# A recurrence with an FFN behind it on one core: v's first product on 128 rows, late transposes by DMA, and a new order of work

## The chip, the core and the metric

The kernel runs on one core of a Trainium2 chip. The core has TensorE (PE in the profile; its weight loads are PEld), VectorE (DVE), ScalarE (ACT), GpSimd (POOL) and SyncE (SP), and 16 DMA engines. The metric is the device time of one execution in microseconds; the median of several runs is compared.

## The reference

Inputs r, k, v, w, a, b are [4 batches, 8 heads, 768 steps, 40], float32. For each of the 32 heads a 40 x 40 state runs through the steps, and its readings go through a feed-forward network (FFN) with 320 inputs, 2048 hidden units and a squared relu:

```python
for t in range(S):
    y[:, :, t] = np.einsum('bhd,bhde->bhe', rt, state)
    Sa = np.einsum('bhde,bhe->bhd', state, at)
    state_decay = state * wt[:, :, None, :] - np.einsum('bhd,bhe->bhde', Sa, bt)
    state = state_decay + np.einsum('bhd,bhe->bhde', vt, kt)
...
h = x @ w_in            # x: y of all heads side by side, [3072, 320]
r = np.maximum(h, 0.0)
return (r * r) @ w_out
```

## The kernel before

The 768 steps are cut into 12 chunks of 64 (`L`, `NCH`). Inside a chunk the recurrence is written as products of 64 x 64 triangles, so that only one small state passes from chunk to chunk. Steps or features of two heads, or of two halves of the heads (g = 0 and 1), share the 128 partitions. For each chunk c the functions run in this order:

- `load(c)` brings w, k, b, a, v and r from HBM on SP's queue (`ldw`, `ldk`, `ldb`, `lda`, `ldv`, `ldr`), in pieces of 160 KB. Chunk 0 also loads the FFN's weights in pieces (`lwi`, `lwl`, `lwo`), which `cwi`, `cwl`, `cwo` cast.
- `prep(c)` takes the logarithm of w (`ln`), splits it (`hi`, `lo`), sums it over the steps on TensorE (`ci`, `cf`) and takes exponentials (`ei`, `ex`, `ef`). `mulKB` scales k and b into the tile KB. `castV` puts v into one half of the rows of VU; u comes into the other half later. `TK` turns KB on TensorE into PSUM and `tK` evicts it into KBT; `TA` and `TR` do so for a and r (tile AR). The triangle `EN` is a product of KBT and AR, and `mEN` masks it into the tile EN (line 689).
- `rec(c)` is the chain from chunk to chunk: `AS` (a times the state) and `EV` (EN times v) add up in one PSUM bank, `u0` evicts it to NZ, `NU` multiplies EN by NZ, `u1` evicts u into VU, `S` and `SC` make the new state and `s` scales it into STb (line 781). `TS` turns the state and `tS` evicts it into Sb, which only the reading of the next chunk needs. EV reads 64 rows of EN and of VU at a time, those that hold v.
- `read(c)` turns VU (`TV`, evicted by `tV` into VUT), makes the triangle `CX` and its masked form `mCX`, adds `RS` (r times Sb) and `Y`, scales the result (`y`, `yd`) and turns it (`XT`, `xt`).
- `ffn(c)` makes h in four parts u (`F` and `FL`), evicts with relu (`f`, lines 928 and 930), squares (`q`) and multiplies by WOUT (`O`), evicts (`o`) and stores (`st`) on SP's queue.

A transpose is a TensorE product with an identity, by `tp` (line 394) or, for the chunks in `WHOLE`, by `tpw` (line 397) on 128 x 128 blocks; all other products are recorded at line 390. Evictions go through `copy_alts` (lines 371 to 380).

The order of the work is not found at run time. `plan.add` collects the operations with what they read and write, and `plan.issue(ORDER)` emits them one by one as the text `ORDER` says, each with its engine (`ACT f 0 u1`) and, on TensorE, the PSUM slot (`PE2 EV 0`, one of four). Every engine runs its own instructions in that order, and waits for the data or for the buffer of an instruction that is not done. A DMA is issued by the engine on whose queue it stands: SP for nearly all, ScalarE for half of the first load and two of the last stores.

Of the kernel before, what the change touches and what calls it, by code (L numbers as in the profile page):

```python
# [8 lines left out]
BF16 = mybir.dt.bfloat16  # L9
# [77 lines left out]
ORDER = """SP ldw 0; SP ldk 0; SP ldb 0; SP ldw 1; ACT ln 0; DVE hi 0; DVE lo 0; SP lda 0; PE0 cf 0; POOL  # L87
castB 0; SP ldk 1; POOL castK 0; ACT eg 0; PE1 TK 0; SP ldb 1; ACT ln 1; PE2 ci 0; DVE tK 0 g0;
ACT ef 0; SP ldv 0; DVE tK 0 g1; POOL hi 1; ACT exw 0; ACT castA 0; SP lda 1; DVE lo 1; PE1 TA 0;
ACT castB 1; PE2 ci 1; SP ldw 2; DVE tA 0 g1; DVE tA 0 g0; PE0 EN 0 g1; ACT exw 1; PE1 cf 1; POOL  # L90
castV 0 g1; DVE mEN 0 g1; ACT castK 1; SP ldr 0; POOL castV 0 g0; PE2 EN 0 g0; ACT ef 1; PE3 BK 0;
DVE mEN 0 g0; SP ldb 2; ACT castA 1; SP lda 2; PE2 EV 0; DVE bK 0; PE0 TA 1; ACT u0 0; SP ldv 1;
DVE tA 1 g1; ACT eg 1; PE NU 0; PE3 TK 1; POOL castR 0; ACT u1 0 g0; DVE tK 1 g0; ACT ln 2; PE1 TR
0; ACT u1 0 g1; POOL hi 2; DVE tA 1 g0; SP lwi 0 k1 x2; ACT tRw 0; POOL lo 2; DVE tK 1 g1; SP ldk
2; PE2 EN 1 g0; PE0 TV 0; ACT castB 2; DVE mEN 1 g0; POOL castA 2; SP ldw 3; PE3 S 0 g0; ACT tV 0;
PE S 0 g1; PE1 EN 1 g1; POOL castV 1 g1; DVE s 0 q0; PE2 BK 1; DVE s 0 q1; ACT castV 1 g0; PE0 ci
2; SP lwi 0 k0 x2; DVE mEN 1 g1; PE3 CX 0 g1; SP lwi 0 k1 x1; ACT exw 2; SP ldr 1; ACT castK 2;
DVE mCX 0 g1; PE0 cf 2; PE1 TK 2; ACT eg 2; SP lwi 0 k0 x3; PE3 AS 1; ACT ef 2; PE EV 1; SP lwi 0
k1 x0; DVE tK 2 g1; SP lwi 0 k0 x0; ACT bK 1; PE0 TS 0; DVE u0 1; SP lwi 0 k1 x3; SP lwi 0 k0 x1;
DVE tK 2 g0; ACT ln 3; PE NU 1; SP ldv 2; ACT tS 0; PE2 CX 0 g0; POOL hi 3; DVE mCX 0 g0; PE1 TA  # L100
2; POOL lo 3; SP lwl 0; ACT u1 1 g0; PE0 SC 1; DVE tA 2 g1; ACT u1 1 g1; PE S 1 g0; PE2 Y 0; DVE
tA 2 g0; POOL castR 1; SP ldk 3; PE S 1 g1; DVE y 0; PE3 TR 1; PE1 EN 2 g1; DVE yd 0; ACT tRw 1;
DVE s 1 q0; POOL cwi 0 k1h0; PE2 EN 2 g0; DVE mEN 2 g1; PE3 TV 1; POOL cwi 0 k0h0; DVE mEN 2 g0;
PE1 BK 2; ACT tV 1; DVE s 1 q1; POOL castV 2 g1; PE2 XT 0; SP lwo 0 x0; POOL castV 2 g0; DVE xt 0;
PE0 ci 3 h0; PE3 ci 3 h1; DVE bK 2; PE2 AS 2; ACT ei 3 h1; PE EV 2; DVE cwi 0 k1h1; POOL cwl 0;
ACT ei 3 h0; PE1 F 0 u0; SP lwo 0 x1; ACT u0 2; ACT ex 3 h0 g0; PE FL 0 u0; SP ldr 2; ACT ex 3 h0
g1; PE NU 2; DVE f 0 u0; ACT ex 3 h1 g0; PE0 CX 1 g1; ACT ex 3 h1 g1; ACT cwi 0 k0h1; SP lda 3;
PE3 FL 0 u1; DVE u1 2 g0; PE F 0 u1; DVE mCX 1 g1; ACT u1 2 g1; PE1 SC 2; SP ldb 3; PE S 2 g0; ACT
f 0 u1; PE2 cf 3; DVE cwo 0 x0; PE0 CX 1 g0; ACT ef 3; PE S 2 g1; DVE mCX 1 g0; POOL cwo 0 x1; PE3
TV 2; PE2 TS 1; DVE s 2 q0; ACT tV 2; SP lwo 0 x2; DVE s 2 q1; PE0 F 0 u2; DVE tS 1; SP lwo 0 x3;  # L110
PE FL 0 u2; ACT castR 2; SP ldv 3; PE1 RS 1; PE Y 1; ACT castA 3; PE2 FL 0 u3; ACT f 0 u2; PE F 0
u3; DVE mulKB 3 h0; POOL mulKB 3 h1; PE3 TA 3; DVE y 1; ACT f 0 u3; PE0 TR 2; DVE yd 1; DVE tA 3
g0; PE1 XT 1; ACT tRw 2; SP ldr 3; PE2 TK 3; DVE xt 1; ACT cwo 0 x2; DVE tA 3 g1; POOL cwo 0 x3;
PE1 FL 1 u1; DVE tK 3; SP ldw 4; PE F 1 u1; POOL q 0 u1; PE3 CX 2 g1; ACT f 1 u1; PE0 CX 2 g0; DVE
mCX 2 g1; PE2 F 1 u2; ACT castV 3 g0; POOL castV 3 g1; SP lwo 0 x4; PE FL 1 u2; DVE mCX 2 g0; PE3
EN 3 g0; ACT f 1 u2; PE1 F 1 u0; POOL castR 3; SP lwo 0 x5; DVE mEN 3 g0; POOL q 0 u0; PE0 EN 3
g1; SP ldk 4; PE FL 1 u0; PE2 RS 2; DVE mEN 3 g1; PE Y 2; PE3 AS 3; ACT ln 4; ACT f 1 u0; PE0 FL 1
u3; DVE hi 4; PE EV 3; DVE yd 2; DVE lo 4; PE F 1 u3; ACT u0 3; POOL cwo 0 x4; DVE y 2; SP lda 4;
PE NU 3; ACT f 1 u3; PE2 ci 4 h0; POOL cwo 0 x5; DVE u1 3 g0; PE1 TS 2; ACT ex 4 h0 g1; SP ldb 4;
POOL q 0 u2; ACT ei 4 h0; DVE u1 3 g1; PE0 O 0 u0; ACT ex 4 h0 g0; ACT tS 2; PE2 ci 4 h1; POOL q 0  # L120
u3; PE3 TV 3; SP lwo 0 x6; ACT ex 4 h1 g0; ACT ei 4 h1; PE1 SC 3; DVE tV 3; ACT ex 4 h1 g1; SP lwo
0 x7; PE S 3 g0; PE S 3 g1; POOL castA 4; SP ldw 5; PE2 TR 3; DVE s 3 q1; PE O 0 u1; ACT tRw 3;
DVE s 3 q0; POOL mulKB 4 h0; PE3 XT 2; PE2 CX 3 g0; ACT xt 2; PE1 cf 4; DVE mCX 3 g0; PE O 0 u2;
ACT ef 4; SP ldv 4; DVE mulKB 4 h1; ACT cwo 0 x6; PE2 TA 4; PE1 CX 3 g1; POOL cwo 0 x7; DVE tA 4
g1; PE3 TK 4; DVE tA 4 g0; POOL q 1 u1; ACT tK 4; PE O 0 u3; DVE mCX 3 g1; PE2 F 2 u0; SP ldw 6;
DVE o 0; ACT q 1 u2; PE3 F 2 u2; DVE q 1 u0; ACT ln 5; PE0 EN 4 g0; PE FL 2 u2; DVE mEN 4 g0; PE1
FL 2 u3; POOL hi 5; ACT f 2 u2; PE FL 2 u0; SP ldr 4; PE F 2 u3; POOL lo 5; ACT f 2 u0; PE3 RS 3;
# [89 lines left out]
def kernel(  # L217
# [12 lines left out]
    nc = tc.nc  # L230
# [856 lines left out]
```

## Time and profile before

| what | value |
|---|---|
| three runs | 249.15, 245.44, 247.75 us, median 247.75 |
| profiled execution, its own time | 245.21 us |
| its span, first to last instruction | 242.8 us |
| TensorE busy | 223.2 us, 5584 products |
| VectorE busy | 182.8 us |
| ScalarE busy | 178.8 us |
| GpSimd busy | 119.9 us |
| granted TensorE clock, mean | 0.993 |
| DMA | 33.54 MB, mean 138 GB/s |

The span is what the trace covers; the execution's own time is 2.4 us longer. In a row of a group the numbers behind the bar are the busy time in us, the mean of one instruction in ns, and the idle time of its engine before it. In a row of the timeline the start and the duration come first.

### The profile page before, as it was taken

The numbers are of one execution on the slowest core, as the hardware profiler recorded it, in microseconds if no ns is written. First come the engines' busy times: TensorE is split into PE (matmuls) and PEld (weight loads), VectorE is DVE, ScalarE is ACT, GpSimd is POOL, SyncE is SP. The second block draws the span as 40 slices with busy tenths as digits, with TensorE's granted clock in tenths as the row PEclk, the third lists the DMA queues.
The fourth block names the chain that finished last, engine by engine and source line by source line (L and its number), as shares of the span: only waits on it lengthen the run. The fifth ranks groups of instructions, "written<-read, shape, count | busy, mean of one in ns | idle before, by whom it ended". The sixth has DMA issues, their size and how long they took to land.

```text
span 242.8 us, 12250 instructions
## 1 busy us (share of the span) xinstructions
PE 223.2 (92%) x5584; PEld 175.7 (72%) x5584; DVE 182.8 (75%) x227; ACT 178.8 (74%) x231; POOL 119.9 (49%) x110
## 2 busy tenths in 40 slices
PE   0587698899999999999999999999999999999994
PEld 0366597588777877777878877777878788787773
DVE  8587869698959875979879877887886876972451
ACT  3478795797788797989879987646798967386560
POOL 8524234319586799764223895609966700330000
PEclk9999979999999999999999999999999999999999
DMA  6989899989978979997864957788457020000403
GB/s 144 232 165 211 191 248 188 227 186 209 196 182 135 196 160 185 184 178 143 173 113 95 223 117 121 186 143 153 106 109 136 6 57 5 3 5 0 100 11 107
DMA packets 102248, 33.54 MB, mean 138 GB/s; under 512 B 89014, under 2 KB 101814, under 8 KB 101942
## 3 DMA queue, kind: packets, MB, share of 16 engines
q1 hardware_dynamic: 101014, 32.45, 64.9%
q8 instruction: 43, 0.70, 1.3%
q10 hardware_dynamic: 1184, 0.33, 0.6%
q14 instruction: 7, 0.06, 0.1%
HBM read 28.84 MB, written 3.93 MB: 135 GB/s over the span
## 4 chain that ended last, share of the span: by engine, by line
PE 77%; SPq 9%; DMA 5%; ACT 2%; issue 2%; POOL 2%; DVE 1%; POOLq 0%; ACTq 0%
PE pb L390 66%; PE pb L394 7%; PE pb L397 4%; SPq L1003 2%; SPq L1011 2%; DMA raw_w<-in_w_dram 2%; DMA CX<-in_moe_w_in_dram 2%; SPq L453 2%; SPq L413 1%; SPq L421 1%; DMA raw_r<-in_r_dram 1%; DVE EN L689 1%; SPq L436 1%; POOL lo L384 1%; DVE CX L689 1%
## 5 line engine op out<-in xcount | busy, mean ns | idle before, releaser
L936 POOL TENSOR_TENSOR G<-G 128x1024 bf16<-128x1024 bf16 x24 | 45.7, 1909 | 32.2 <-ACT G L928 29.9
L390 PE MATMUL pb<-WOUT,G 128*128 128x320 bf16 (+1 forms) x400 | 57.0, 294 | 0.0
L928 ACT ACTIVATE G<-pb 128x1024 bf16<-128x1024 f32 x39 | 39.5, 1022 | 15.4 <-PE pb L390 15.3
L390 PE MATMUL pb<-XT,WIN 128*128 128x256 bf16 x384 | 48.4, 273 | 0.0
L390 PEld LDWEIGHTS <-G 128*128 128x128 bf16 x400 | 36.3, 98 | 13.7 <-issue 0.8
L390 PEld LDWEIGHTS <-WIN 128*128 128x128 bf16 x384 | 34.7, 98 | 8.1 <-issue 3.6
L689 DVE TENSOR_TENSOR CX<-pb,MSKI 128x1024 bf16<-128x1024 f32 x24 | 29.0, 1219 | 5.5 <-PE pb L390 5.4
L689 DVE TENSOR_TENSOR EN<-pb,MSK 128x1024 bf16<-128x1024 f32 x24 | 28.9, 1218 | 3.2 <-PE pb L390 3.0
L384 POOL TENSOR_TENSOR KB<-raw_kb,iG 128x640 bf16<-128x640 f32 x13 | 21.3, 1641 | 9.0 <-DMA raw_kb<-in_b_dram 8.3
L781 DVE TENSOR_TENSOR STb<-pb,GT 64x640 bf16<-64x640 f32 x22 | 18.0, 820 | 2.7 <-PE pb L390 2.4
L658 DVE TENSOR_TENSOR AR<-pb,GT 128x512 bf16<-128x512 bf16 x24 | 15.7, 686 | 5.2 <-PE pb L394 2.4
L384 POOL TENSOR_TENSOR lo<-lnW,hi 128x640 bf16<-128x640 f32 x9 | 13.2, 1466 | 11.4 <-ACT hi L376 11.0
L574 ACT ACTIVATE Gin<-pb 64x320 f32<-64x320 f32 x36 | 15.5, 429 | 4.3 <-PE pb L390 3.8
L390 PE MATMUL pb<-XT,WLAST 64*128 64x256 bf16 x192 | 17.1, 271 | 0.6 <-POOL WLAST L380 0.4
L390 PEld LDWEIGHTS <-EN 64*64 64x64 bf16 x768 | 14.8, 112 | 2.7 <-issue 1.6
L376 ACT ACTIVATE AR<-pb 128x512 bf16<-128x512 bf16 (+1 forms) x17 | 11.4, 694 | 6.7 <-PE pb L394 2.9
L859 DVE TENSOR_TENSOR Yb<-pb,Gin 128x640 bf16<-128x640 f32 (+1 forms) x24 | 12.4, 550 | 4.1 <-PE pb L390 4.1
L938 ACT ACTIVATE G<-G 128x1024 bf16<-128x1024 bf16 x15 | 15.5, 1052 | 0.0
L390 PE MATMUL pb<-UTI,hi 64*128 64x64 bf16 x192 | 8.2, 198 | 8.0 <-DVE hi L371 7.5
L930 DVE TENSOR_SCALAR G<-pb 128x1024 bf16<-128x1024 f32 x9 | 11.0, 1220 | 5.3 <-PE pb L390 5.3
L568 ACT ACTIVATE iG<-pb 128x640 f32<-128x640 f32 x18 | 12.5, 700 | 2.7 <-PE pb L390 2.5
L380 POOL CAST hi<-lnW 128x640 bf16<-128x640 f32 x7 | 5.0, 719 | 18.2 <-ACT lnW L532 9.5
(114 smaller groups left out, 446.5 us busy)
## 6 DMA issues: line engine op xcount, KB each, us to landing
raw_kb<-in_k_dram SPq DMA_DIRECT2D x24, 160.0 KB, 4.4
raw_kb<-in_b_dram SPq DMA_DIRECT2D x24, 160.0 KB, 4.5
raw_a<-in_a_dram SPq DMA_DIRECT2D x24, 160.0 KB, 3.9
raw_v<-in_v_dram SPq DMA_DIRECT2D x24, 160.0 KB, 4.7
raw_w<-in_w_dram SPq DMA_DIRECT2D x23, 160.0 KB, 4.9
raw_r<-in_r_dram SPq DMA_DIRECT2D x22, 160.0 KB, 4.2
out_dram<-osb SPq DMA_DIRECT2D x22, 160.0 KB, 3.3
osb<-in_moe_w_out_dram SPq DMA_DIRECT2D x8, 320.0 KB, 6.1
```

The lines of the kernel that those rows point to most:

```text
L384: return [("POOL", 40 + 2.35 * n, lambda: nc.gpsimd.tensor_tensor(out=o_(), in0=a_(), in1=b_(), op=op)), ("DVE", c_dve(n), lambda: nc.vect ...
L390: return lambda: nc.tensor.matmul(out=o_(), lhsT=l_(), rhs=r_(), start=start, stop=stop, skip_group_check=True)
L394: return lambda: nc.tensor.transpose(out=o_(), in_=i_(), identity=IDb[rows(g), :])
L568: ew(f"ei {c} h{jh}", [("ACT", c_act(2 * n), lambda hb=hb, jh=jh: nc.scalar.activation(out=iG[0][:].rearrange("p (g j) e -> p g (j e)", g= ...
L574: nc.scalar.activation(out=Gin[c % NGI][rows(g), NP * jh:NP * jh + NP, :].rearrange("p j e -> p (j e)"), in_=slot(hb, FP32)[rows(g), g, 0: ...
L658: ew(f"tA {c} g{g}", [("DVE", c_dve(512), lambda g=g: nc.vector.tensor_tensor(out=steps(AR[q2][:, 0, g]), in0=turned(ha, g), in1=steps(GT[ ...
L689: evac(f"m{nm} {c} g{g}", lambda s, n: [("DVE", c_dve(n), lambda: nc.vector.tensor_tensor(out=dst[q2][:, g, s].rearrange("p q i t -> p (q ...
L781: ew(f"s {c} q{q}", [("DVE", c_dve(2 * n), lambda q=q: nc.vector.tensor_tensor(out=STb[q2][rows(q), :, q, 0:D], in0=slot(hs, FP32)[rows(q) ...
L859: return [("DVE", c_dve(2 * (f1 - f0)), lambda: nc.vector.tensor_tensor(out=Yb[q2][:, :, to:to + f1 - f0], in0=slot(hy, FP32)[:, :, f0:f1] ...
L928: ("ACT", c_act(1024), lambda gb=gb, hf=hf: nc.scalar.activation(out=gb, in_=slot(hf, FP32)[:], func=ACTF.Relu)),
L936: ("POOL", 1900, lambda gv=gv: nc.gpsimd.tensor_tensor(out=gv, in0=gv, in1=gv, op=ALU.mult)),
L938: ("ACT", c_act(1024), lambda gv=gv: nc.scalar.activation(out=gv, in_=gv, func=ACTF.Square))],
```

## The change

Five things change together.

1. For chunks 3 to 11 (`EVC`) the product EV reads all 128 rows of EN and VU in place of the 64 that hold v. The rows of VU that will hold u are set to zero before, by the new operations `zu` on GpSimd or VectorE, and EV is put in the tile form C (128 rows, 64 columns) in place of Q (64 rows, 64 columns).
2. For chunks 5 to 11 (`DTK`) KB is turned by a transposing DMA on ScalarE's queue (`dK`) straight into KBT, in place of `TK` and `tK`.
3. For chunks 8 to 11 (`DTV`) VU is turned in the same way (`dV`), in place of `TV` and `tV`.
4. For chunks 8 to 10 (`DTS`) the state is turned in the same way (`dS`), in place of `TS` and `tS`. Sb has 64 columns a head in place of 40 for that; a transposing DMA turns sixteen blocks of 128 x 128 bf16, 512 KB, from SBUF to SBUF.
5. `ORDER` is new throughout: engines of 137 operations differ, and so do the order of the loads on SP's queue, the place of the FFN's weights among them and the PSUM slots.

```diff
+    DTK, DTV, DTS = range(5, 12), range(8, 12), range(8, 11)
+    EVC = range(3, 12)
...
-    Sb = buf("Sb", [128, NJ, 2, D], BF16, 2)
+    Sb = buf("Sb", [128, NJ, 2, 64], BF16, 2)
...
+    def turn(name, out_, in_, reads, writes):
+        plan.add(name, [("ACT", 1300)], ("ew", {"ACT": lambda: nc.scalar.dma_start_transpose(
+            out=out_(), in_=in_())}), reads=reads, writes=writes)
...
-        if c not in RUNS:
+            if c in EVC:
+                ew(f"zu {c} g{g}", [(e, d, lambda q=q, g=g: q.memset(
+                    VU[c % NK][rows(g), NJ * g:NJ * g + NJ, :], 0.0))
+                    for e, d, q in (("POOL", 700, nc.gpsimd), ("DVE", 500, nc.vector))],
+                   writes=[("VU1", c % NK, g)])
+
+        if c in DTK:
+            turn(f"dK {c}", lambda: KBT[q2][:].rearrange("p j x t -> p j (x t)"),
+                 lambda: KB[c % NK][:].rearrange("p h e -> p (h e)"), KBK, [("KBT", q2)])
+        if c not in RUNS and c not in DTK:
             hb = ("A", "TK", c)
...
-                                 lambda p=p, q=q, g=g: EN[q2][rows(1 - g), g, q, p, :],
-                                 lambda p=p, q=q, g=g: vu[rows(1 - g), NJ * g + 2 * p + q, 0:D],
+                                 lambda p=p, q=q, g=g: (EN[q2][:, g, q, p, :] if c in EVC else
+                                                        EN[q2][rows(1 - g), g, q, p, :]),
+                                 lambda p=p, q=q, g=g: vu[:, NJ * g + 2 * p + q, 0:D]
+                                 if c in EVC else vu[rows(1 - g), NJ * g + 2 * p + q, 0:D],
                                  c == 0 and p % 4 == 0 and q == 0, False))
-        pe(f"EV {c}", "Q", 40, ms, reads=both(("EN", q2, 0), ("EN", q2, 1)) + VU0,
+        VU1 = [("VU1", c % NK, 0), ("VU1", c % NK, 1)]
+        pe(f"EV {c}", "C" if c in EVC else "Q", 40, ms,
+           reads=both(("EN", q2, 0), ("EN", q2, 1)) + VU0 + (VU1 if c in EVC else []),
            writes=[hb], alloc=[hb] if c == 0 else [])
...
+            if c in DTS:
+                turn(f"dS {c}", lambda: Sb[q2][:].rearrange("p i q e -> p i (q e)"),
+                     lambda: STb[q2][:].rearrange("p i q e -> p (i q e)"),
+                     [("STb", q2, 0), ("STb", q2, 1)], [("Sb", q2)])
+                return
             ht = ("A", "TS", c)
...
+        if c in DTV:
+            turn(f"dV {c}", lambda: VUT[q2][:].rearrange("p j x t -> p j (x t)"),
+                 lambda: vu[:].rearrange("p h e -> p (h e)"), VU0 + VU1, [("VUT", q2)])
+        else:
+            hb = ("A", "TV", c)
...
```

The beginning of SP's part of `ORDER`, before and after, and where the transposing DMAs stand in ScalarE's part:

```
SP before: ldw 0; ldk 0; ldb 0; ldw 1; lda 0; ldk 1; ldb 1; ldv 0; lda 1; ldw 2; ldr 0; ldb 2; lda 2; ldv 1; lwi 0 k1 x2; ldk 2; ...
SP after:  ldw 0; lda 0; ldk 0; ldv 0; ldb 0; lda 1; ldw 1; ldk 1; ldw 2; lwi 0 k1 x1; ldb 1; ldr 0; lwi 0 k1 x3; ...
DVE before: hi 0; lo 0; tK 0 g0; tK 0 g1; lo 1; tA 0 g1; tA 0 g0; mEN 0 g1; mEN 0 g0; bK 0; tA 1 g1; ...
DVE after:  hi 0; castK 0; tK 0 g0; tA 0 g0; tA 0 g1; tK 0 g1; lo 1; castK 1; mEN 0 g0; mEN 0 g1; bK 0; tA 1 g1; ...
ACT after:  ... f 2 u0; dK 5; q 1 u1; ... u0 5; dK 6; tR 5 g0; ...
```

More of the change, by code (lines that the diff above doesn't have):

```diff
@@ L86 @@
 O_AFTER = 0
[L87 to L103, printed above, removed]
@@ L110 @@
[L110 to L115, printed above, removed]
@@ L122 @@
[L122 to L127, printed above, removed]
@@ L212 @@
[L212 to L213 removed]
+ORDER = """SP ldw 0; SP lda 0; SP ldk 0; SP ldv 0; ACT ln 0; DVE hi 0; POOL lo 0; SP ldb 0; DVE castK 0; PE0
+cf 0; SP lda 1; ACT ef 0; SP ldw 1; POOL castV 0 g0; ACT castA 0; PE1 TA 0; ACT castB 0; SP ldk 1;
+ACT eg 0; PE2 TK 0; POOL castA 1; SP ldw 2; PE3 ci 0; DVE tK 0 g0; DVE tA 0 g0; ACT ln 1; SP lwi 0
@@ new lines @@
+DVE s 0 q0; DVE tRw 0; PE0 EN 1 g1; ACT tV 0; PE1 cf 2; DVE mEN 1 g1; SP ldr 2; PE2 EN 1 g0; ACT
+castV 1 g0; PE3 AS 1; DVE mEN 1 g0; POOL castK 2; PE0 CX 0 g1; ACT castV 1 g1; SP ldv 2; POOL
+castA 2; ACT ef 2; DVE castB 2; PE2 BK 1; DVE mCX 0 g1; ACT eg 2; PE EV 1; SP lwi 0 k0 x0; PE0 TK
+2; ACT bK 1; DVE u0 1; SP lwi 0 k0 x2; PE1 TA 2; DVE tK 2 g1; SP ldr 1; PE NU 1; PE2 TS 0; ACT u1
+1 g0; DVE tA 2 g0; SP lda 3; DVE tA 2 g1; POOL castV 2 g0; ACT tS 0; DVE tK 2 g0; PE1 EN 2 g1; SP
+ldw 4; ACT u1 1 g1; PE2 ci 2; DVE mEN 2 g1; PE0 SC 1; ACT exw 2; PE3 EN 2 g0; PE S 1 g0; ACT ln 3;
```

254 lines of the change are left out of this document (137 added, 117 removed).

## The prediction

> **What bounds the kernel now.** I read the page's first and fourth parts, then the stretches before and after the start-up, then what TensorE waited for.
>
> ```profile
> span 242.8 us, 12250 instructions
> PE 223.2 (92%) x5584; PEld 175.7 (72%) x5584; DVE 182.8 (75%) x227; ACT 178.8 (74%) x231; POOL 119.9 (49%) x110
> PE 77%; SPq 9%; DMA 5%; ACT 2%; issue 2%; POOL 2%; DVE 1%; POOLq 0%; ACTq 0%
> ...
> core 0: us, PE busy (x) PEld busy (x) DVE busy (x) ACT busy (x) POOL busy (x), PEclk, DMA share, GB/s
> 0.00:46.00 46.00, 30.80 (x794) 24.95 (x794) 35.71 (x54) 29.64 (x36) 21.22 (x35) 0.96 0.93 196
> 46.00:239.00 193.00, 192.04 (x4789) 150.61 (x4789) 147.08 (x173) 148.82 (x196) 98.67 (x76) 1.00 0.61 125
> 80.00:220.00 140.00, 139.65 (x3825) 109.36 (x3825) 110.61 (x129) 110.09 (x149) 79.57 (x60) 1.00 0.60 120
> ...
> PE pb L390 <- POOL WLAST L380: 0.4, 1, 0.4
> PE pb L390 <- issue: 0.2, 1, 0.2
> PE pb L390 <- DVE EN L689: 0.2, 1, 0.2
> ```
>
> The kernel has two halves with different limits. From 46 to 239 us TensorE works 192.04 of 193 us, and the last three rows (what it waited for from 46 us on) come to 0.8 us: here every product removed shortens the run, as long as nothing new makes TensorE wait. In the first 46 us it works only 30.8 us while the DMA engines are 93% busy: this half is set by loads and by the dependent chain of the first chunks, and fewer products bring nothing there. The transposes removed belong to the second half; the new order changes both.
>
> **The transposes leave TensorE: -6.6 us.** Seven groups TK (chunks 5 to 11), four TV (8 to 11) and three TS (8 to 10) go, 32 products each, 448 of 5584. The timeline shows the length of a group as the distance of starts:
>
> ```profile
> 94.60 0.64 PE L394 MATMUL pb<-IDb,STb 64*128 64x64 bf16 x32
> 95.08 0.19 PE L390 MATMUL pb<-UTI,hi 64*128 64x64 bf16 x2
> ...
> 95.78 0.63 PE L394 MATMUL pb<-IDb,VU 64*128 64x64 bf16 x32
> 96.25 0.63 PE L394 MATMUL pb<-IDb,KB 64*128 64x64 bf16 x32
> ```
>
> TS takes 95.08 - 94.60 = 0.48 us, TV 96.25 - 95.78 = 0.47 us. 14 x 0.47 = 6.6 us, all of it in the full half. TensorE can give no more than this.
>
> **EV on 128 rows: 0.** It has 32 products before and after, of 40 columns. The two forms stand side by side in the groups, EV now and Y, which has the form that EV gets:
>
> ```profile
> L390 PE MATMUL pb<-VU,EN 64*64 64x40 bf16 x384 | 8.5, 187 | 0.1
> L390 PE MATMUL pb<-KB,CX 128*64 128x40 bf16 x384 | 8.0, 186 | 0.1
> ```
>
> 187 against 186 ns each. That EV follows AS in the same tile form may save something at the seam; nine chunks at no more than 0.1 us either way give ±0.9 us, and I take 0.
>
> **The clearing of v's other half and the moved evictions: +1.0 us.** EV now waits for `zu`, 18 memsets of 64 x 1024 bf16.
>
> ```profile
> L320 POOL MEMSET STb<- 128x2048 bf16 x2 | 3.6, 1805 | 0.4 <-POOLq L1071 0.3
> L318 DVE MEMSET KB<- 128x384 uint32 x3 | 1.1, 378 | 0.1
> L371 DVE COPY KBT<-pb 128x2048 bf16<-128x2048 bf16 x7 | 8.5, 1219 | 2.3 <-PE pb L394 2.3
> L376 ACT ACTIVATE KBT<-pb 128x2048 bf16<-128x2048 bf16 x2 | 3.7, 1874 | 0.6 <-PE pb L394 0.6
> L376 ACT ACTIVATE VUT<-pb 128x2048 bf16<-128x2048 bf16 x6 | 11.3, 1876 | 3.4 <-PE pb L397 1.7 <-PE pb L394 1.6
> L371 DVE COPY Sb<-pb 128x1280 bf16<-128x1280 bf16 x5 | 4.1, 823 | 3.2 <-PE pb L394 2.9 <-PE pb L397 0.3
> L928 ACT ACTIVATE G<-pb 128x1024 bf16<-128x1024 f32 x39 | 39.5, 1022 | 15.4 <-PE pb L390 15.3
> L930 DVE TENSOR_SCALAR G<-pb 128x1024 bf16<-128x1024 f32 x9 | 11.0, 1220 | 5.3 <-PE pb L390 5.3
> L376 ACT ACTIVATE NZ<-pb 128x640 bf16<-128x640 f32 x9 | 6.3, 705 | 3.4 <-PE pb L390 3.4
> L376 ACT ACTIVATE VU<-pb 64x640 bf16<-64x640 f32 x13 | 9.0, 696 | 1.6 <-PE pb L390 1.3 <-DVE VU L373 0.2
> L373 DVE TENSOR_SCALAR VU<-pb 64x640 bf16<-64x640 f32 x11 | 9.0, 818 | 1.7 <-PE pb L390 1.6
> ```
>
> Eleven run on POOL at half of 1805, 0.9 us each; POOL is idle half of the time, so nothing. Seven run on VectorE at 378 x 512 / 384 = 0.5 us, 3.5 us. The new order also hands operations over, counted engine by engine in the two lists. ScalarE loses 2 KBT and 4 VUT evictions (11.2 us), 7 of G (7.2), 4 of NZ (2.8) and some 7 us of casts and r evictions, and gains 6 VU (4.2) and some 4 us of small ones: about -20 us. VectorE loses 5 KBT, 3 Sb and 6 VU (13.5) and some 3 us of small ones, and gains 7 of G (8.5), 4 of NZ (3.3), the memsets and some 7 us: about +6 us, to 189 of 243 us. The cover is VectorE's idle quarter (147 of 193 us busy in the full half); it is not idle where a product waits, so I charge a sixth, 1.0 us (bounds 0 and 6).
>
> **Fourteen transposing DMAs on ScalarE's queue: +4.0 us.** No row shows such a DMA. Each reads and writes 512 KB inside the chip's SBUF, and its issue holds everything behind it on ScalarE: the G evictions that free PSUM, the exponentials of the next chunk, `u1`. It also waits there for KB from POOL and VectorE, or for VU. The nearest rows are issues of loads:
>
> ```profile
> 2.95 1.24 SPq L421 DMA_DIRECT2D raw_kb<-in_b_dram  x2
> ...
> 35.45 5.12 SPq L1003
> ...
> raw_kb<-in_b_dram SPq DMA_DIRECT2D x24, 160.0 KB, 4.5
> ```
>
> A free queue takes a 160 KB piece in 1.24 / 2 = 0.62 us; a 256 KB piece against full DMA engines held its queue 5.12 us. These are the bounds. 512 KB is 3.2 pieces, 3.2 x 0.62 = 2.0 us, which I take. Then ScalarE gets 14 x 2.0 = 28 us for the 20 us it loses, +8 us in a stretch (80 to 220 us) where it is idle 140 - 110.1 = 29.9 us. By sums it fits. But a held ScalarE frees PSUM later, and TensorE has no slack; I charge half, 4.0 us. At 0.6 us an issue it is 0; at 5.12 us ScalarE gets 71.7 - 20 = 51.7 us, and what exceeds the idle 29.9 is 21.8 us on the path.
>
> The landing, 4.5 us for 160 KB, may be 5 to 8 us for 512. Between a `dK`, `dV` or `dS` and the first product that reads it the new order leaves 8 to 13 us of other TensorE work (`dK 8` to `EN 8`: three groups O, two F, `S`, `SC`, `TV` and small ones). That work hides it: 0. If it is gone, a late KBT stops EN, then the masked EN, then EV of that chunk.
>
> [...]
>
> **DMA time: +1.0 us.** At the best slice of the page, 248 GB/s, 14 x 512 KB take 14 x 2.1 = 29 us of all engines, in a stretch where they are 60% busy. Loads there are prefetched and no TensorE wait names one, so it is cover enough up to about 5 us of late loads; I take 1.0.
>
> **The new order in the start-up: +6.0 us.** The first loads leave SP in another order: w, a, k, v, b of chunk 0, then a and w of chunk 1; before it was w, k, b, w, a.
>
> ```profile
> 5.60 2.26 SPq L443 DMA_DIRECT2D raw_a<-in_a_dram  x2
> 10.47 1.33 SPq L436 DMA_DIRECT2D raw_v<-in_v_dram  x2
> ...
> 7.72 1.82 POOL L380 CAST tKB<-raw_kb 128x640 bf16<-128x640 f32 x2 [0.84 <-DMA raw_kb<-in_b_dram]
> ...
> 9.60 1.03 PE L394 MATMUL pb<-IDb,tKB 64*128 64x64 bf16 x32 [0.26 <-POOL tKB L380]
> 10.75 2.36 DVE L512 TENSOR_TENSOR KBT<-pb,iG 128x1024 bf16<-128x1024 bf16 x2 [2.44 <-PE pb L394]
> 13.02 0.81 DVE L386 TENSOR_TENSOR lo<-lnW,hi 128x640 bf16<-128x640 f32 x1
> 14.40 1.29 DVE L658 TENSOR_TENSOR AR<-pb,GT 128x512 bf16<-128x512 bf16 x2 [0.57 <-PE pb L397]
> 16.08 2.50 DVE L689 TENSOR_TENSOR EN<-pb,MSK 128x1024 bf16<-128x1024 f32 x2 [0.39 <-PE pb L390]
> ```
>
> b of chunk 0 ended POOL's wait at 7.72. Behind a (1.2 to 2.26 us) and v (1.33) it comes 2.5 to 3.6 us later, 10.2 to 11.3; one cast of 0.73, and TK starts at 11 to 12 in place of 9.60. VectorE then does two halves of KBT (2.36), AR twice (1.29), `lo 1` (0.81) and, new, `castK 1` (about 0.8) before the first masked EN: 12.0 + 1.15 + 5.3 = 18.4 us against 16.08, 2.3 us late. Chunk 1 repeats it: its b stands eleventh on SP, behind two weights and a piece of the FFN's weights, in place of seventh, some 3 to 4 us later, and VectorE gets `tRw 0`, `tRw 1` and `castB 2` from ScalarE. TensorE has nothing else to do then, since WIN is not there yet. 2.3 + 3.7 = 6.0. The other way: the last third of w_in is loaded earlier, and with it the 0.4 us wait for WLAST and the 1.6 us of idleness around it may go; bounds -1.6 and +8.
>
> **Sum.** -6.6 + 0 + 1.0 + 4.0 + 0 + 1.0 + 6.0 = +5.4 us: span 248.2. The profiled execution took 245.21 us, 2.4 outside its span, so 250.6 for its like. It was the fastest of its kind; the three runs shown go from 245.44 to 249.15 with median 247.75, and the predicted median is 247.75 + 5.4 = 253.2 us.
>
> **The rivals.**
> *ScalarE's queue is held.* Issue near 5.12 us, or a queue that pushes back: 21.8 us in place of 4.0, so 271 us. For it: ScalarE is the engine that frees most of FFN's PSUM, and POOL's G waits on it. It decides from about 3.5 us an issue, where 14 x 3.5 - 20 = 29 us eats the idle time. [...]
> *The start-up costs nothing and the issues are short.* -6.6 + 1 and nothing else: 242.2 us. For it: 46 to 239 us is all TensorE. Against it: b's place in SP's order is a fact of the lists.
> *The gain and the start-up cancel.* Issues at 0.6 us, start-up +6, the rest +1: 248 us.
> *The transposes do not leave TensorE.* Excluded: the program has 448 products fewer.
>
> **How the numbers follow.** Forecast 0.45, held queue 0.18, cheap start 0.15, cancelled 0.22. The likeliest is 253.2 us; its own range, from the start-up's 4 to 8 and the issue's 1 to 8, is 248 to 260. For 8 in 10 it must reach most of the held queue and the edge of the cheap start: 243.5 to 270. 2% is 5 us, about what a measurement of this kernel can tell from no change: below 242.8 lies most of the cheap start, 0.15; 242.8 to 252.7 takes the cancelled case and a fifth of the forecast, 0.30; above, 0.55.
>
> **What would show it.** Right: about 5136 products; TensorE idle in the first 46 to 60 us grown from 15 us to over 20; first TK near 12 us; issues of 2 us on ScalarE's queue. Wrong: a start-up as dense as before; issues under 1 or over 3.5 us; in the full half, TensorE waiting for KBT, VUT or Sb, which would mean late landings.

## The result, and the profile after

| kernel | median us | lowest to highest | ratio to before, 95% interval |
|---|---|---|---|
| before | 247.04 (4 runs) | 245.44 to 249.15 | 1 |
| changed | 262.71 (4 runs) | 260.89 to 263.05 | 1.0668 [1.0616, 1.072] |

The ratios leave out runs that were disturbed, so a ratio below need not be the quotient of the medians beside it. The change costs 16.5 us (6.7 % of 247.04). The forecast was +5.4. The profiled execution took 263.05 us, its span 261.3 (242.8 before).

The page's first part, and its row of ScalarE's DMA queue:

```profile
span 261.3 us, 11365 instructions
PE 222.6 (85%) x5136; PEld 171.6 (66%) x5136; DVE 192.8 (74%) x236; ACT 159.6 (61%) x216; POOL 127.1 (49%) x120
...
q10 hardware_dynamic: 30304, 7.67, 19.0%
```

448 products are gone as announced (5584 to 5136), and ScalarE computes 19.2 us less (178.8 to 159.6; the forecast said about 20). Yet TensorE stands for 38.7 us of its span in place of 19.6. The table by stretches says where (columns: length, busy PE, PEld, DVE, ACT and POOL, granted clock, DMA share, GB/s):

```profile
0.00:46.00 46.00, 27.65 (x724) 23.00 (x724) 36.13 (x53) 27.46 (x32) 16.62 (x29) 0.89 0.96 207
46.00:80.00 34.00, 31.25 (x756) 25.41 (x750) 25.51 (x31) 29.91 (x42) 18.65 (x18) 1.00 0.92 185
80.00:220.00 140.00, 127.28 (x3123) 95.50 (x3120) 112.30 (x132) 84.94 (x124) 84.23 (x70) 0.99 0.89 152
```

The row of before for the middle stretch, which was not shown yet:

```profile
46.00:80.00 34.00, 33.39 (x781) 26.61 (x780) 28.79 (x35) 28.37 (x37) 19.10 (x16) 1.00 0.89 189
```

In the first 46 us TensorE idles 18.4 us (15.2 before), to 80 us another 2.8 (before, 33.39 of 34 busy: 0.6), and from 80 to 220 us 12.7 (0.35). So 5.3 us were lost in the start, and 12.4 in the stretch that had been full. What TensorE waited for from 80 us on (total, times, longest):

```profile
PE pb L397 <- ACT G L956: 3.5, 1, 3.5
PE pb L393 <- ACT G L956: 3.0, 3, 1.4
PE pb L393 <- ACT Gin L581: 2.1, 2, 2.0
PE pb L393 <- ACT AR L379: 1.3, 1, 1.3
PE pb L393 <- issue: 1.3, 1, 1.3
PE pb L393 <- ACT Sb L379: 0.7, 1, 0.7
```

Nearly every row names a computing instruction of ScalarE: evictions of G, of Gin, of AR. No row names a transposing DMA; the one row with Sb is ScalarE's own eviction into it, of a chunk that is still turned on TensorE. ScalarE has got work taken off and is late all the same. The transposing DMAs themselves, by their line (issue time, shortest, median, longest):

```profile
L474 ACTq DMA_TRANSPOSE KBT<-KB x7: 1927/2990/3935, 91.1 to 210.9; - x7
L474 ACTq DMA_TRANSPOSE VUT<-VU x4: 1806/3058/3841, 174.2 to 226.8; - x4
L474 ACTq DMA_TRANSPOSE Sb<-STb x3: 2021/3099/3145, 187.7 to 229.5; - x3
```

And ScalarE's timeline at the costliest place, with what TensorE does behind it:

```profile
194.06 1.02 ACT L956 ACTIVATE G<-pb 128x1024 bf16<-128x1024 f32 x1
197.16 3.67 ACTq L474 DMA_TRANSPOSE VUT<-VU  x1
200.88 1.94 ACT L956 ACTIVATE G<-pb 128x1024 bf16<-128x1024 f32 x2 [5.80 <-issue]
...
197.75 0.71 PE L393 MATMUL pb<-XT,WIN 128*128 128x256 bf16 x5
201.95 0.41 PE L397 MATMUL pb<-IDb,tR 64*128 64x64 bf16 x16 [3.49 <-ACT G L956]
```

The eviction that began at 194.06 ended at 195.08. ScalarE then did nothing for 2.08 us, spent 3.67 in the issue, and only at 200.88 evicted the two parts of h whose PSUM banks TensorE wanted: 3.49 us of idle TensorE for one transposing DMA. Below, a transposing DMA is called a turn, after the function that adds it, and a time in which ScalarE gets nothing else done because of one, the wait ahead of it and its issue, is called a stand.

### The profile page after: what moved, and what is told of

Its sections match the earlier page's. It is cut to its first block, busy times and chain, and to the rows that moved or that the text cites. A ratio compares the mean times of both kernels' runs of the same rounds, so it can differ in the third digit from the quotient of the medians.

```text
span 261.3 us, 11365 instructions
## 1 busy us (share of the span) xinstructions
PE 222.6 (85%) x5136; PEld 171.6 (66%) x5136; DVE 192.8 (74%) x236; ACT 159.6 (61%) x216; POOL 127.1 (49%) x120
## 5 line engine op out<-in xcount | busy, mean ns | idle before, releaser
L964 POOL TENSOR_TENSOR G<-G 128x1024 bf16<-128x1024 bf16 x23 | 43.5, 1892 | 42.8 <-DVE G L958 22.1
L393 PE MATMUL pb<-XT,WIN 128*128 128x256 bf16 x384 | 50.1, 276 | 0.2
L956 ACT ACTIVATE G<-pb 128x1024 bf16<-128x1024 f32 x32 | 32.2, 1020 | 25.3 <-PE pb L393 16.6
L958 DVE TENSOR_SCALAR G<-pb 128x1024 bf16<-128x1024 f32 x16 | 19.5, 1221 | 14.1 <-PE pb L393 13.4
L387 POOL TENSOR_TENSOR KB<-raw_kb,iG 128x640 bf16<-128x640 f32 x12 | 19.0, 1583 | 17.2 <-ACT iG L575 7.9
L379 ACT ACTIVATE VU<-pb 64x640 bf16<-64x640 f32 x19 | 13.3, 698 | 17.9 <-PE pb L393 9.5
L966 ACT ACTIVATE G<-G 128x1024 bf16<-128x1024 bf16 x16 | 16.5, 1052 | 8.2 <-DVE G L958 3.7
L393 PEld LDWEIGHTS <-EN 64*64 64x64 bf16 (+1 forms) x768 | 15.2, 114 | 3.4 <-issue 2.7
L597 ACT ACTIVATE GT<-pb 128x1024 f32<-128x1024 f32 x12 | 12.2, 1020 | 7.9 <-PE pb L393 7.2
L383 POOL CAST VU<-raw_v 64x640 bf16<-64x640 f32 x18 | 14.0, 776 | 3.7 <-DMA raw_v<-in_v_dram 2.9
```

Of the source, the lines that this page charges most:

```text
L379: alts.append(("ACT", c_act(n), lambda: nc.scalar.activation(out=o_(), in_=i_(), func=ACTF.Copy, scale=1.0 if scale is None else scale)))
L383: lambda: nc.gpsimd.tensor_copy(out=o_(), in_=i_())))
L387: return [("POOL", 40 + 2.35 * n, lambda: nc.gpsimd.tensor_tensor(out=o_(), in0=a_(), in1=b_(), op=op)), ("DVE", c_dve(n), lambda: nc.vect ...
L393: return lambda: nc.tensor.matmul(out=o_(), lhsT=l_(), rhs=r_(), start=start, stop=stop, skip_group_check=True)
L956: ("ACT", c_act(1024), lambda gb=gb, hf=hf: nc.scalar.activation(out=gb, in_=slot(hf, FP32)[:], func=ACTF.Relu)),
L958: ("DVE", c_dve(1024), lambda gb=gb, hf=hf: nc.vector.tensor_scalar(out=gb, in0=slot(hf, FP32)[:], scalar1=0.0, scalar2=None, op0=ALU.max))],
```

## The experiments

Times are set against the kernel before on the same chip, whose median was 245.9 to 246.5 us there; one per cent is 2.5 us. Where I give microseconds they are a difference of two ratios times 246.5. Most of these ratios are known to 0.5 to 1 % either way, 1.2 to 2.5 us, and a difference of two to somewhat less.

### Is it the transposing DMAs, and what of them?

**No turns.** `turn` emits nothing. KBT, VUT and Sb of the late chunks keep old contents.

```diff
-        plan.add(name, [("ACT", 1300)], ("ew", {"ACT": lambda: nc.scalar.dma_start_transpose(
-            out=out_(), in_=in_())}), reads=reads, writes=writes)
+        plan.add(name, [("ACT", 0)], ("ew", {"ACT": lambda: None}), reads=reads, writes=writes)
```

> The changed kernel with the fourteen transposing DMAs left out; KBT, VUT and Sb keep what earlier chunks put there, so that part of the computation is missing. Order, engines, EV on 128 rows and zu are those of the changed kernel. Theory H (the issues hold ScalarE, evictions come late, TensorE stalls) and rival D (the turns' packets slow the loads) both expect about 249 us: before's 247, less 6.2 of products, plus 6.4 of the start, plus 1 to 2 of order. Rival O (the new order stalls TensorE in the full half by itself) expects over 257 us.

Measured 252.07 us, ratio 1.0153 [1.0053, 1.0253]. Without turns 80 to 220 us is nearly full again:

```profile
80.00:220.00 140.00, 137.57 (x3374) 103.93 (x3372) 121.12 (x143) 89.45 (x129) 84.77 (x70) 1.00 0.61 119
```

The turns cost 5.15 %, 12.7 us (9.9 by the quotients of the medians). What is left, 1.5 %, is the net of the start, the zeroing and the order against the products that are gone.

**All turns on SyncE's queue**, in the same places of the written order:

```diff
-        plan.add(name, [("ACT", 1300)], ("ew", {"ACT": lambda: nc.scalar.dma_start_transpose(
+        plan.add(name, [("SP", 1300)], ("ew", {"SP": lambda: nc.sync.dma_start_transpose(
```

> The changed kernel with all fourteen transposing DMAs on SyncE's queue at the same places of the order; the computation is whole. H: ScalarE is free, TensorE no longer waits for evictions behind an issue, 249 to 253 us, with a few us lost where SyncE's queue waits for KB or VU and holds loads. D: the packets are the same, so it stays at 260 us or more.

Measured 250.93 us, ratio 1.0201 [1.0112, 1.029]: 11.5 us better than the changed kernel, with the same fourteen transfers, and not told apart from no turns at all.

```profile
L474 SPq DMA_TRANSPOSE KBT<-KB x7: 1928/2917/3608, 92.1 to 199.8; - x7
...
80.00:220.00 140.00, 137.05 (x3368) 103.49 (x3366) 120.20 (x143) 89.52 (x129) 84.70 (x70) 1.00 0.95 168
```

The issue is as slow there (2.9 us), and the DMA engines are even busier than in the changed kernel (0.95 from 80 to 220 us against 0.89), but TensorE is served. DMA load by itself as the cause is refuted.

**One block a turn**: the same fourteen issues for a sixteenth of the bytes.

```diff
-            out=out_(), in_=in_())}), reads=reads, writes=writes)
+            out=out_()[:, 0, :], in_=in_()[:, 0:128])}), reads=reads, writes=writes)
```

> The changed kernel, each transposing DMA turning one 128x128 block in place of sixteen; the other blocks keep what earlier chunks put there. H with an issue that grows with the size: under 1 us an issue, the run near 249 us. H with an issue that is fixed for one DMA: issues stay near 2 to 3 us and the run at 260 us or more. D expects near 249 us, since a sixteenth of the packets is left.

Measured 257.46 us, ratio 1.047 [1.0394, 1.0545]: neither answer. The issues fell to 1.1 us, but here is the place of above:

```profile
187.05 1.02 ACT L956 ACTIVATE G<-pb 128x1024 bf16<-128x1024 f32 x1
194.09 1.13 ACTq L474 DMA_TRANSPOSE VUT<-VU  x1
195.27 1.94 ACT L956 ACTIVATE G<-pb 128x1024 bf16<-128x1024 f32 x2 [7.20 <-issue]
...
190.49 0.46 SPq L466 DMA_DIRECT2D raw_r<-in_r_dram  x1
```

ScalarE stood for 6.0 us *before* the issue, though all that this turn reads had been ready since 185.5. In the trace of the changed kernel the 207 DMAs issued on both queues raise eight semaphores, 25 or 26 DMAs each, and ahead of 188 of the issues stands a wait for the same semaphore that the DMA then raises. In the compiled program of this run the turn waits so for the 7 x 320 piece of the load of r of chunk 11, of which the last row shows the issue: SyncE had kept that load until its buffer came free (ahead of the same load it waited 8.2 us for GpSimd's cast of r in the changed kernel). In the changed kernel the turn of 197.16 shares its semaphore with the same piece, which SyncE issued at 194.89, and the semaphore was last raised at 197.06: the 2.08 us of nothing ahead of the turn are this wait as well, as far as the trace tells.

**One block a turn, without that wait**: the load of r of chunk 11 goes behind that of chunk 10 in SyncE's list, which gives the turn another predecessor.

```diff
-... SP ldr 11; ... SP st 5; ... SP ldv 11; ... SP ldr 10; ...
+... SP st 5; ... SP ldv 11; ... SP ldr 10; SP ldr 11; ...
```

> The one-block kernel (each turn moves one block of 128x128 in place of sixteen, so k over b, v over u and the state are wrong past their first block) with one SyncE entry moved: the load of r for chunk 11 goes behind the load of r for chunk 10. In the one-block kernel ScalarE stood from 188.1 to 194.09 us before it issued the turn of v over u of chunk 9, and in the compiled program that turn waits for a semaphore which a 7x320 piece of that load of r raises; after the move it waits for the turn of the state of chunk 8, which landed some 10 us before. Theory S (the stand before this turn, for a transfer that the turn has no use for, is what kept the one-block kernel 5.4 us above the kernel without turns): ScalarE goes from the eviction ahead of the turn straight to the turn, and the time falls by 4 to 6 us to 252 to 253. Theory F (the fixed cost of an issue, fourteen times 1.1 us, is what kept it there): the stand goes and the time stays at 256 to 258.

Measured 250.77 us, ratio 1.0193 [1.0115, 1.0271], 6.8 us less by the ratios, and ScalarE no longer stands. The turn goes out at 186.59, and the eviction behind it (189.18) now waits for TensorE:

```profile
186.59 1.20 ACTq L474 DMA_TRANSPOSE VUT<-VU  x1
187.02 1.02 ACT L956 ACTIVATE G<-pb 128x1024 bf16<-128x1024 f32 x1
189.18 1.02 ACT L956 ACTIVATE G<-pb 128x1024 bf16<-128x1024 f32 x1 [1.15 <-PE pb L393]
```

So fourteen stands of about 1.1 us cost nothing to speak of (1.0 us over no turns, within the intervals), and one stand of 6 us cost nearly seven. TensorE waited 4.9 us for the eviction behind that stand, and then ran at a lower clock (0.66, the column ahead of the DMA share; 10.00 x 0.34 is 3.4 us of work at full clock):

```profile
192.00:202.00 10.00, 5.65 (x117) 4.03 (x117) 2.81 (x3) 4.37 (x7) 3.33 (x3) 0.66 0.48 103
```

### Is ScalarE's stand enough, with no transfer?

**Even stands, no DMA.** In the kernel without turns ScalarE makes two copies of the turn's source into a scratch tile where the turn was; again KBT, VUT and Sb are not written.

```diff
+        def hold():
+            for n in (2048, 1024):
+                nc.scalar.activation(out=SCR[:, 0:n], in_=in_()[:, 0:n], func=ACTF.Copy, scale=1.0)
+        plan.add(name, [("ACT", 2900)], ("ew", {"ACT": hold}), reads=reads, writes=writes)
```

> The kernel without turns (252.1 us; k over b, v over u and the state of the late chunks are not turned, as in that run), with ScalarE occupied in the place of each turn by two copies of the turn's source into a scratch tile, 128x2048 and 128x1024: by the evictions of that size (128x1024 in 1.02 us, two of them in 1.94) about 2.9 us each, as long as a turn's issue took on average (2.9 us), with no transfer at all. Theory H (the loss to the turns is ScalarE standing in the issue, whatever the transfer does): 260 to 263 us, as the changed kernel has. Theory D (the transfers, on the DMA engines or at the memory, do the harm too): 252 to 256 us.

Measured 257.28 us, ratio 1.0459 [1.0392, 1.0526]: between the two answers, 7.5 of the 12.7 us.

**Stands as long as measured.** The same, with one to three copies a turn, as long as ScalarE stood at that turn in the changed kernel, the waits ahead of the issue counted in.

```diff
-            for n in (2048, 1024):
+            for n in HOLD[name]:   # dK 8: 2048; dV 8: 2048, 2048, 1367; dV 9: 2048, 2048, 2048; ...
```

> The kernel without turns, with ScalarE occupied in the place of each turn by copies of the turn's source, now as long as ScalarE stood at that turn in the profile of the changed kernel, its wait before the issue counted in (from 1.8 us for v over u of chunk 10 to 5.1 for v over u of chunk 8 and 5.75 for that of chunk 9; 44.6 us in all, where the run with 2.9 us each had 41.5). Theory L (a stand costs by what it has over the slack of the products behind it, so that the few long ones make up what the even ones did not show): 260 to 263 us, the whole loss of the changed kernel. Theory D (beside ScalarE's stand the transfers themselves cost some 5 us): 257 to 258, as with the even stands.

Measured 264.03 us, ratio 1.0713 [1.0658, 1.0767]: 13.8 us, where the turns cost 12.7, without one transposing DMA. (By the quotients of the medians the even stands cost 5.3 us, these 11.8 and the turns 9.9: the same order.) Even the waits return, one by one (TensorE from 80 us on):

```profile
PE pb L394 <- ACT G L961: 3.5, 3, 1.9
PE pb L398 <- ACT G L961: 3.3, 1, 3.3
PE pb L394 <- ACT Gin L586: 2.4, 2, 2.2
PE pb L394 <- ACT AR L380: 1.4, 1, 1.4
...
196.42 5.79 ACT L479 ACTIVATE SCR<-VU 128x2048 bf16<-128x2048 bf16 x3
202.12 1.92 ACT L961 ACTIVATE G<-pb 128x1024 bf16<-128x1024 f32 x2
```

3.5, 3.3, 2.4 and 1.4 us, against 3.0, 3.5, 2.1 and 1.3 in the changed kernel. Some 3 us more of standing in all (44.6 against 41.5), put where the long ones were, cost 6.3 us more. Part of that is the clock, 0.98 in the mean from 80 to 220 us against 1.00 with even stands (140 x 0.02 = 2.8 us). The rest agrees with theory L of the expectation; the slack of the products behind each stand was not measured.

**One turn less on ScalarE**: only that of v over u of chunk 9 goes to SyncE.

```diff
+        e, queue = ("SP", nc.sync) if name == "dV 9" else ("ACT", nc.scalar)
```

> The changed kernel with one of its fourteen turns, that of v over u of chunk 9, on SyncE's queue in its place (ScalarE stood 5.75 us at it; behind it TensorE waited 3.55 us for an eviction and ran at half clock for 3.4 us). Theory L: this one turn gives back the wait and the clock, 4 to 6 us: 257 to 259. Rival (the loss is spread evenly over the turns): under 1 us, 261.5 to 262.5.

Measured 262.18 us, ratio 1.0617 [1.0551, 1.0684]: 1.3 us less than the changed kernel by the ratios, with intervals that overlap. The expected 4 to 6 us did not come. The profiled execution, the longest of the four, no longer has the wait of 3.5 us, but TensorE still idles 11.2 us from 80 to 220 us, against 12.7 in the changed kernel. The stand of one turn can be the place where TensorE waits, and still give little when it goes alone; whether the next stands took the wait over, this run does not settle.

### The start

**The kernel before, with the 141 entries ahead of BK 2 in the changed order and on its engines** (SyncE's entries shown).

```diff
-SP ldw 0; SP ldk 0; SP ldb 0; SP ldw 1; SP lda 0; ...
+SP ldw 0; SP lda 0; SP ldk 0; SP ldv 0; SP ldb 0; ...
```

> The kernel before, with the operations that stand ahead of BK 2 in its order (the first 141 of 1032) put into the changed kernel's order and on its engines; everything behind BK 2 as before, no transposing DMA. Theory S (the new start costs 6 us): 251 to 253 us, first TK near 12 us, EV 0 near 22 us. Rival (the start's delay is absorbed, since loads and the FFN's weights set the first 46 us anyway): within 1 us of the kernel before, 247 us.

Measured 250.71 us, ratio 1.0186 [1.0099, 1.0273], +4.6 us: a real cost, a little under the 251 to 253 us that the first theory named. This kernel too is sewn from two orders, and its TensorE idles 1.9 us more than before between 46 and 220 us, so some of the 4.6 us may belong to the seam.

**The other way round**, with the turns on SyncE's queue and the start put back up to the middle of chunk 3:

```diff
-SP ldw 0; SP lda 0; SP ldk 0; SP ldv 0; ACT ln 0; DVE hi 0; POOL lo 0; SP ldb 0; ...
+SP ldw 0; SP ldk 0; SP ldb 0; SP ldw 1; ACT ln 0; DVE hi 0; DVE lo 0; SP lda 0; ...   (up to S 3 g0)
```

> The changed kernel with two things put back: all turns on SyncE's queue (as in the run with them there, 250.9 us), and the instructions that lead up to the state product of chunk 3 (S 3 g0) in the order, on the engines and in the accumulator slots of before. Theory (the rest of the loss is the new start order, which cost 4.3 us when it was put alone into the kernel before): the first 46 us hold 30 to 31 us of products as before does, and the time is 250.9 - 4.3 = 246.6, 245 to 248. Rival (what is left is the new order behind the start, which in the kernel without turns left TensorE 2.4 us idle from 80 to 220 us): the time stays at 250 to 252.

Measured 252.58 us, ratio 1.0303 [1.0208, 1.0397]: nothing came back. A start from one order sewn to a middle from another makes a seam:

```profile
46.00:80.00 34.00, 28.41 (x708) 22.86 (x708) 24.71 (x31) 25.19 (x33) 13.58 (x14) 1.00 0.91 189
```

TensorE idles 5.6 us between 46 and 80 us, where the kernel with all turns on SyncE's queue idles 2.9. What the start may have given back, the seam may have taken; this run does not tell them apart. A shorter piece put back is told of below.

### v's first product on 128 rows

**Alone, in the order of before**, the eighteen `zu` each behind its `castV`, and no turn:

```diff
+    DTK, DTV, DTS = (), (), ()
+    EVC = range(3, 12)
+... ACT castV 3 g0; DVE zu 3 g0; ...
```

> The order of before, with v's first product on all 128 rows in chunks 3 to 11 and the zeroing of the u half that this needs (eighteen instructions, on the engines that the change gives them, each right behind the cast of v of its half); no turn, no other move. The forecast gave the product 0 (bounds 0.9 either way) and the zeroing and moved evictions +1.0 (0 to 6.0). Theory as forecast: 0 to +1.5 us, 247 to 248.5. [...] Rival (zeroing on VectorE and GpSimd holds evictions): +3 or more, 250 and up.

Measured 248.86 us, ratio 1.0113 [1.0046, 1.018], +2.8 us, close to the rival's 3 and above the forecast's 1.5. The product is neither faster nor slower, and the clearings are as long as forecast:

```profile
L626 POOL MEMSET VU<- 64x1024 bf16 x11 | 10.4, 945 | 0.6
L395 PE MATMUL pb<-VU,EN 128*64 128x40 bf16 (+1 forms) x384 | 8.4, 188 | 0.0
L626 DVE MEMSET VU<- 64x512 uint32 x7 | 3.4, 485 | 0.8 <-issue 0.3
```

But TensorE idles 3.6 us from 46 to 80 us in place of 0.6, and 2.65 us from 80 to 220 us in place of 0.35. The longest waits in both stretches are for VectorE and GpSimd, the engines that got the clearings; that the clearings made them late is the likely reading, not a shown one (first two rows: 46 to 80 us):

```profile
PE pb L395 <- DVE Yb L889: 1.3, 1, 1.3
PE pb L395 <- DVE CX L706: 1.0, 1, 1.0
...
PE pb L399 <- POOL KB L389: 1.0, 1, 1.0
PE pb L395 <- DVE XT L376: 0.4, 2, 0.3
```

**Taken back in the new order**, with the turns on SyncE's queue:

```diff
-    EVC = range(3, 12)
+    EVC = ()
-... POOL zu 4 g0; ... DVE zu 3 g1; ...
```

> The kernel with turns on SyncE's queue (250.9 us), with v's first product of chunks 3 to 11 as before (on 64 rows) and the eighteen zeroings left out. If the two edits add up: 250.9 - 2.8 = 248.1 us, 247 to 249.5. If the zeroing is hidden in the new order, which leaves VectorE and GpSimd other gaps: 250 to 252.

Measured 252.25 us, ratio 1.022 [1.0155, 1.0285], against 1.0201 [1.0112, 1.029] with it: nothing came back. That the new order leaves VectorE and GpSimd other gaps and hides the clearing there is the expectation's reading and was not shown.

**Then a shorter piece of the start put back too**, up to the second half of E and N of chunk 2:

```diff
-SP ldw 0; SP lda 0; SP ldk 0; SP ldv 0; ACT ln 0; DVE hi 0; POOL lo 0; SP ldb 0; ...
+SP ldw 0; SP ldk 0; SP ldb 0; SP ldw 1; ACT ln 0; DVE hi 0; DVE lo 0; SP lda 0; ...   (up to EN 2 g0)
```

> The kernel of the run just above, with the entries ahead of the second half of E and N of chunk 2 (EN 2 g0, 31 of TensorE's entries) in the order, on the engines and in the slots of before, and nothing put back behind them: a shorter piece than the one that did not help, which ended in the middle of chunk 3. If the start's 4.3 us can be had back: 243 to 245 us, faster than before by about 1 %. If only half comes back, since the rest of the start stays as changed: 245 to 247. If the start and the order behind it only work together: 248 or more.

Measured 250.47 us over all ten runs, ratio 1.0075 [1.0011, 1.0139]: 3.6 us less than the run above it by the ratios, 1.8 us by the medians. It fits the third answer, 248 or more. With the 4.6 us of the first run of the start, that term is seen from both sides, but its size is known only to 2 or 3 us.

### Can the products saved be had?

**The long start put back, and entries moved to come earlier.** The two written orders differ in 247 places, far more than the forty that the expectation names.

```diff
-... ACT castV 2 g1; ... DVE s 1 q1; ... SP lwo 0 x1; ...
+... SP lwo 0 x1; ... ACT castV 2 g1; ... DVE s 1 q1; ...
```

> The kernel with turns on SyncE's queue and the old start, with some forty entries of its written order moved by a few places so that evictions and turns come earlier ahead of the products that wait for them; the same instructions. If the products saved by the turns (6.2 us of TensorE's work) can be had once no turn stands on ScalarE and the order leaves no new waits: 240 to 244 us, faster than before by 1 to 3 %. If TensorE's start and PSUM slots bind whatever the order: 246 to 248.

Measured 255.04 us, ratio 1.0335 [1.0248, 1.0422]. Nothing was gained; TensorE idles 7.6 us from 80 to 220 us.

**The order of before nearly to the state product of chunk 4, many entries moved behind it, seven turns (k over b of chunks 8 to 11, the state of 8 to 10) on SyncE's queue:**

```diff
-    DTK, DTV, DTS = range(5, 12), range(8, 12), range(8, 11)
-    EVC = range(3, 12)
+    DTK, DTV, DTS = (8, 9, 10, 11), (), (8, 9, 10)
+    EVC = ()
```

> The order of before up to the state product of chunk 4 untouched, v's first product as before, and only seven turns, k over b of chunks 8 to 11 and the state of chunks 8 to 10, all on SyncE's queue, with entries behind that point moved by some places so that the turns have landed when their products come; seven transposes and their evictions fewer. If the products saved can be had without the new start and without ScalarE: 243 to 245.5 us, up to 1 % faster than before. If new waits take it back: 247 or more.

Measured 247.08 us, ratio 1.0045 [1.0015, 1.0075]: half a per cent slower than before.

```profile
PE 220.2 (91%) x5360; PEld 173.0 (71%) x5360; DVE 179.8 (74%) x222; ACT 176.2 (73%) x229; POOL 120.1 (49%) x110
...
80.00:220.00 140.00, 137.55 (x3605) 107.12 (x3606) 107.49 (x126) 109.36 (x149) 79.98 (x60) 1.00 0.81 148
...
PE pb L392 <- ACT G L955: 1.4, 1, 1.4
PE pb L392 <- DMA KBT<-KB: 0.4, 1, 0.4
...
198.65 1.86 SPq L473 DMA_TRANSPOSE KBT<-KB  x1
...
204.81 0.41 PE L392 MATMUL pb<-AR,KBT 64*128 64x64 bf16 x16 [0.37 <-DMA KBT<-KB]
```

Seven groups of 32 products gone took 3.0 us off TensorE's busy time (223.2 to 220.2), and 3.1 us of new idleness, 2.1 of it from 80 to 220 us, took them back. No version that was run beats the kernel before.

## Why the prediction was wrong, step by step

The direction was right, and the time lay in the wide range of 243.5 to 270 us, but above the 248 to 260 us that the forecast gave for itself; the size was wrong by 11 us.

- **The transposes leave TensorE, -6.6: right in size.** The last run gives 3.0 us of busy time for seven groups, where 7 x 0.47 = 3.3 was forecast. For all fourteen it comes out only as a sum. The new start put in alone raises TensorE's busy time by 2.4 us (to 225.6) and the clearing alone by 1.1 (to 224.3); 223.2 + 2.4 + 1.1 - 6.6 = 220.1, and the runs without turns, with turns on SyncE and with one block without the wait have 220.7, 219.9 and 219.5. Why the changed kernel itself has 222.6 was not shown.
- **EV on 128 rows, 0: right** (187 to 188 ns). **The clearing and the moved evictions, +1.0 (0 to 6):** the clearing cost 2.8 us alone in the old order, and nothing to be seen in the new one; the moved evictions were not run alone. VectorE's work grew by 10.0 us (182.8 to 192.8), not by 6. Inside its bounds.
- **Fourteen transposing DMAs on ScalarE's queue, +4.0: this is the step that failed.** It measured 11.5 us (to SyncE's queue) to 12.7 (no turns). Two things in it were wrong. First, the length: 2.0 us an issue was taken from a free queue, and the trace has 1.81 to 2.01 in the three issues under 40 % DMA load, but 2.76 to 3.94 in nine of the ten over 95 %; and ahead of three issues ScalarE waited, 3.9 us in all, for GpSimd or for the predecessor on a semaphore. ScalarE stood 44.5 us, not 28. Second, the sum: ScalarE's load was set against its idle time over 140 us, as if a stand could be spread. In these runs it could not: the one with even stands and the one with uneven ones differ by 6.3 us for 3 us of standing. The text named the mechanism (PSUM freed later, no slack in TensorE), then priced it with a share of an average. Half of the measured stand less 20 would have given (44.5 - 20) / 2 = 12.2, which looks right by chance: the same rule gives 10.8 for the even stands, which cost 7.5. Of the 11 us this step has 7.5 to 8.7.
- **The rival of the held queue**, "it decides from about 3.5 us an issue", was the right one with the wrong threshold and price: it decided at a mean of 2.9, at 263 and not 271 us. The sign "wrong: issues under 1 or over 3.5 us" rang for four of the fourteen (3.64 to 3.94), and did not for the mean; the longest stand, wait included, was 5.75 us.
- **The landing, hidden, 5 to 8 us guessed: right.** No wait of TensorE in the changed kernel names it. ScalarE did wait for one: its turn at 174.21 shares a semaphore with the turn of 167.06, and went out 1.24 us after the eviction ahead of it had ended, when that one had landed, 7.1 us after its issue began. In the last run a product waited for a KBT whose issue began at 198.65, and went on at 204.81: 6.2 us. With the turns on SyncE two landings can be timed, 6.1 and 6.8 us after the start of the issue. An issue at little DMA load, at 216.44 with a DMA share of 0.35, took 1.81 us for 512 KB, where 3.2 pieces of a plain load in a free queue take 2.0 (3.2 x 0.62). Under load no run sets the two side by side.
- **DMA time, +1.0: not contradicted.** With the turns on SyncE the run lies 0.5 % (1.2 us) above the one without turns, inside the intervals.
- **The start, +6.0: right in kind, somewhat too big.** 4.6 us put in alone, 3.6 (by the medians 1.8) taken out, and 5.3 us of idle in the first 80 us of the changed kernel. The idle time named as a sign, over 20 us by 46 to 60 us, came to 18.4 and 19.7. The steps came nearly as written: TK at 12.68 (11 to 12 forecast), the first masked EN at 18.43 us (18.4 forecast):

```profile
12.68 1.03 PE L397 MATMUL pb<-IDb,tKB 64*128 64x64 bf16 x32
...
18.43 2.35 DVE L704 TENSOR_TENSOR EN<-pb,MSK 128x1024 bf16<-128x1024 f32 x2
```

- **What the sum lacked.** Without turns the new kernel is 3.8 us slower than before (1.53 % of 246.5), which is -6.6 for the products, +4.6 for the start and 5.8 more, where the forecast had 1.0. That remainder, itself known only to 3 us or so, would be the clearing (0 to 2.8 us) and the new order behind the start, of which 2.1 us show as idleness from 80 to 220 us (2.43 against 0.35). How it divides is not settled. Nor had the sum a term for the clock, 1.7 us behind the wait of 3.49 (last section).

## What to carry to other kernels

Here each issue of 512 KB held ScalarE's queue for 1.8 to 3.9 us, and up to 5.75 us with the wait ahead of it. So count the longest stand against the slack of whoever waits for the next instruction behind it, and not the sum of the stands against the engine's idle time. Try large transfers on the queue of an engine that computes nothing; the same fourteen transfers cost 11.5 us less on SyncE's. And where work is taken off a dense engine, look first at what its products wait for next: in the last run the 3.0 us saved came back as 3.1 us of waiting.

## What was not expected of the hardware

- **The issue of a transposing DMA was longer where the DMA engines were loaded**: in the changed kernel 512 KB took 1.81 to 2.01 us in the three issues under 40 % DMA load, 2.44 at 55 %, and 2.76 to 3.94 in nine of the ten over 95 %. The tenth, the last issue, goes against it: 2.02 us at full load. On SyncE's queue 512 KB took 1.8 to 3.7 us. One block of 32 KB on ScalarE's took 1.1 to 1.9, in the median 1.1 to 1.2.
- **A DMA waited for another queue's unrelated DMA**, by the shared semaphore: ScalarE stood 6.0 us for it in the run with one block a turn, and no longer when one load was moved.
- **The granted clock.** Behind the 3.49 us wait of the changed kernel TensorE was granted 0.50 of its clock from 202.89 to 206.30 us, 0.79 in the mean of the 8 us below, and 0.83 in the mean of 10 us around the like wait (3.3 us) of the run with measured stands (the column ahead of the DMA share):

```profile
200.00:208.00 8.00, 5.76 (x125) 3.86 (x125) 3.36 (x4) 4.78 (x8) 2.78 (x2) 0.79 0.66 131
...
198.00:208.00 10.00, 6.46 (x102) 4.70 (x100) 4.33 (x4) 8.40 (x10) 5.80 (x5) 0.83 0.46 100
```

  By 8.00 x 0.21 that is 1.7 us. In the first 46 us the mean clock was 0.96 before, 0.89 after and 1.00 in the run without turns, whose start is written the same; what sets it there is not settled.
